# Top-32 attention joined to a capacity-dropping mixture of experts: the sign tile multiplied, the loop one unit deeper, reciprocals later, and three smaller edits

## The chip, the cores and the metric

The program runs on one core of a Trainium2 chip. The metric is the device time of one execution in microseconds. Five engines work side by side, each taking its own instructions in order: TensorE (PE, with its weight loads shown as PEld), VectorE (DVE), ScalarE (ACT), GpSimd (POOL) and SyncE (SP, which here only issues DMA). TensorE's results go to PSUM, of which this kernel uses all eight banks in the attention loop.

## The reference, cut to what matters

Attention keeps the 32 largest scores of every query row, and its result feeds a routed expert layer in which every one of eight experts serves at most 80 tokens.

```python
# q, k, v: (8 batches, 8 heads, 576 rows, 64), float32
scores = scale * np.matmul(q, k.transpose(0, 1, 3, 2))
kth = np.partition(scores, -32, axis=-1)[..., -32:-31]       # the 32nd largest of each row
scores = np.where(scores >= kth, scores, -1e9)
attn = np.exp(scores - max); attn /= attn.sum(-1) + 1e-9     # (cut: keepdims)
x = (attn @ v) as (4608 tokens, 512)                         # (cut: transpose, reshape)
# experts: w_gate (512, 8), w1 (8, 512, 1024), w2 (8, 1024, 512), capacity 80
expert = argmax(x @ w_gate); gate = softmax(x @ w_gate)[expert]
for e in range(8):
    tok = the 80 tokens of expert e with the largest gate
    out[tok] = gate[tok] * (relu(x[tok] @ w1[e]) @ w2[e])     # all other rows are zero
```

## The kernel before

The attention works through 32 pairs of heads (n). A pair has five blocks of query rows (t): four of 128 rows, each counted as two units (h = 0, 1, one for each head), and a last block of 64 rows in which both heads share the 128 partitions as one unit. That makes 9 units a pair and 288 units in all. Each unit is a tile of 128 rows by 576 scores, and `step(i)` issues one step of a software pipeline: work for unit i and for its neighbours, each at another stage.

For every unit VectorE must find the 32nd largest score of each row. It takes the 8 largest of six pieces of 96 scores (48 candidates), finds the 24th largest of these, removes from the row everything at or above it (tile y), takes the 8 largest of the rest, and picks the 32nd with the help of a count (cnt) that ScalarE makes.

```python
    def parts(self, i):                       # letter G of the step: six of these (a takes the end)
        for j in range(NG):
            nc.vector.max(out=cand[:, j, :], in_=s[:, j * S // NG : (j + 1) * S // NG])      # L208
            yield

    def search(self, i):                      # letters a b c d e y g h, one part at each yield
        ...
        for r in range(G0 // 8):              # 3 rounds: a, (b) c, (d) e
            nc.vector.max(out=dst, in_=cand)                                                 # L219
            if r == G0 // 8 - 1:              # after e: ScalarE's sign of (24th - s), summed into cnt
                sign = self.rows.tile([P, S], BF16, name="sign", tag="sign", bufs=1)
                nc.scalar.activation(sign, s, Act.Sign, bias=w9[:, 7:8], scale=-1.0, accum_out=cnt)   # L224
            yield
            if r < G0 // 8 - 1:
                nc.vector.match_replace(out=cand, in_to_replace=dst, in_values=cand, imm_value=LOW)   # L227
                yield
        y = self.rows.tile([P, S], F32, name="y", tag="y")
        nc.vector.scalar_tensor_tensor(out=y, in0=s, scalar=w9[:, 7:8], in1=s, op0=Alu.is_lt, op1=Alu.mult)  # L230
        yield                                 # y
        nc.vector.max(out=w9[:, 8:], in_=y)   # g                                             # L232
        yield
        nc.vector.scalar_tensor_tensor(out=pick, in0=past, scalar=cnt, in1=w9[:, 7:], ...)   # h, L235: the threshold
        yield

    def below(self, i):                       # letter m: GpSimd's mask
        nc.gpsimd.tensor_scalar(self.mask[i], self.s[i], self.thr[:, i : i + 1], None, op0=Alu.is_lt)   # L243
```

TensorE and ScalarE do the rest for each block. `front` makes the scores (TensorE into the tile sp, L196; ScalarE copies them to s, L201). `turn_w` turns s (L275) and adds the mask (L280) into the PSUM tiles ab and cc; ScalarE takes the exponential (L282, L284). `back` multiplies by v (L298) into a part of cc, with the row sums beside the products. `over` is VectorE's reciprocal of those sums (L310, the letter z), and `divide` ScalarE's scaling by it (L319). `turn` transposes the next pair's q and k. `norm`, once a pair, transposes the result (L173, L174), multiplies it by the gate weights (L336), and has VectorE add the logits (L345). The tile sp is a single buffer of four banks, and `front`, `turn` and two parts of `norm` all use it in turn.

```python
            back = dict(a=0, b=1, c=1, d=1, e=1, y=1, g=2, h=3, m=3)   # how many units behind each letter works
            for c in "GhmbGcGdGeGGgazy":                                 # VectorE's (and m: GpSimd's) order in a step
                ...
            if whole(i - 3):
                self.turn_w(*units[i - 3][:2])
            for u in drawn: self.divide(*u)                              # (cut)
            fronts = 0 <= i + 3 < NU and units[i + 3][2] != 1
            if not fronts and due: self.turn(due.pop()); busy = True     # (cut)
            for g in list(later): ...                                    # the parts of norm, in steps without front
            if fronts:
                self.front(*units[i + 3][:2])
            if whole(i - 4):
                self.back(*units[i - 4][:2]); drawn.append(...)
```

After the loop come the routing (`route`) and the experts. In the routing, TensorE runs 72 products of a zero tile with itself (L623) while VectorE finds each expert's 80th gate (L660, L662), then a few small products (L667, L676, L677), 48 weight loads with products for the list of chosen tokens (L692), and 36 more zero products. In the experts, `product` ends with one copy of the PSUM tile yp to SBUF, and `store` transposes that copy, scales it and writes the rows out:

```python
        def product(e):
            for d in range(HP):               # 4 column blocks of w2
                ... nc.tensor.matmul(ps[u : u + HF, d, :cap], ...)       # L766
            nc.scalar.copy(y_t[e], ps[:, :, :cap])                      # L769, 128 x 320
        def store(e):
            for d in range(HP):
                nc.tensor.transpose(ps[:cap, d * P : (d + 1) * P], yT[:, d, :], ident)   # L775
```

Of the kernel before, what the change touches and what calls it, by code (L numbers as in the profile page):

```python
# [9 lines left out]
F32 = mybir.dt.float32  # L10
BF16 = mybir.dt.bfloat16
# [15 lines left out]
def kernel(  # L27
# [11 lines left out]
    nc = tc.nc  # L39
# [18 lines left out]
    NG = 6  # L58
    G0 = 24
    TOP = 24  # L60
    WARM1, WARM2 = 72, 36
    UPP = 2 * NF + 1
    NU = NP * UPP

# [58 lines left out]
    class Attention:  # L123
# [62 lines left out]
        def front(self, n, t):  # L186

            qT, kT = self.turned[n]
            m = P if t < NF else TL
            i = n * UPP + 2 * t  # L190
            ps = self.four()
            for j in range(2):
                for h in range(2):
                    d = slice(D * h, D * h + D)
                    o = ps[:, 2 * h + j, :HS] if t < NF else ps[TL * h : TL * h + TL, j, :HS]
                    nc.tensor.matmul(o, lhsT=qT[d, t * P : t * P + m], rhs=kT[d, j * HS : (j + 1) * HS], start=True, stop=True)  # L196
            g = 2 if t < NF else 1
            s = self.rows.tile([P, 2 * S], F32, name="s", tag="s", bufs=2 if self.lean else 4)
            for h in range(g):
                self.s[i + h] = s[:, h * S : (h + 1) * S]  # L200
            nc.scalar.activation(s[:, : g * S].rearrange("p (j c) -> p j c", c=HS), ps[:, : 2 * g, :HS], Act.Copy, scale=TINY)  # L201
# [10 lines left out]
        def search(self, i):  # L212

            s, cand = self.s[i], self.top[i]
            top = self.top[i] = self.small.tile([P, G0 // 8 - 1, 8], F32, name="top", tag="top")
            w9 = self.small.tile([P, 16], F32, name="w9", tag="w9")
            for r in range(G0 // 8):
                dst = top[:, r, :] if r < G0 // 8 - 1 else w9[:, :8]
                nc.vector.max(out=dst, in_=cand)  # L219
                if r == G0 // 8 - 1:  # L220

                    sign = self.rows.tile([P, S], BF16, name="sign", tag="sign", bufs=1)
                    cnt = self.small.tile([P, 1], F32, name="cnt", tag="cnt")
                    nc.scalar.activation(sign, s, Act.Sign, bias=w9[:, 7:8], scale=-1.0, accum_out=cnt)  # L224
                yield
                if r < G0 // 8 - 1:
                    nc.vector.match_replace(out=cand, in_to_replace=dst, in_values=cand, imm_value=LOW)  # L227
                    yield
            y = self.rows.tile([P, S], F32, name="y", tag="y")
            nc.vector.scalar_tensor_tensor(out=y, in0=s, scalar=w9[:, 7:8], in1=s, op0=Alu.is_lt, op1=Alu.mult)  # L230
            yield
            nc.vector.max(out=w9[:, 8:], in_=y)  # L232
            yield
            pick = self.small.tile([P, TOP_K - G0 + 1], F32, name="pick", tag="pick")
            nc.vector.scalar_tensor_tensor(out=pick, in0=past, scalar=cnt, in1=w9[:, 7:], accum_out=self.thr[:, i : i + 1],  # L235
                                           op0=Alu.is_equal, op1=Alu.mult)
            yield

        def below(self, i):

            self.top.pop(i)
            self.mask[i] = self.rows.tile([P, S], BF16, name="mask", tag="mask", bufs=3)
            nc.gpsimd.tensor_scalar(self.mask[i], self.s[i], self.thr[:, i : i + 1], None, op0=Alu.is_lt)  # L243

        def search_all(self, i):

            s = self.s[i]
            top = self.top[i] = self.small.tile([P, TOP_K // 8, 8], F32, name="top", tag="top")
            scr = self.rows.tile([P, S], F32, name="y", tag="y")
            nc.vector.max(out=top[:, 0, :], in_=s)  # L250
            for r in range(1, TOP_K // 8):
                nc.vector.match_replace(out=scr, in_to_replace=top[:, r - 1, :], in_values=s if r == 1 else scr,
                                        imm_value=LOW)
                nc.vector.max(out=top[:, r, :], in_=scr)
            nc.vector.tensor_copy(self.thr[:, i : i + 1], top[:, TOP_K // 8 - 1, 7:8])
# [125 lines left out]
        def run(self, slow):  # L381

            units = []
            for n in range(NP):
                for t in range(NF):
                    units += [(n, t, 0), (n, t, 1)]
                units.append((n, NF, 2))
            first, second = {}, {}
            later = []
            due = []  # L390
            drawn = []
            ready = {}

            def whole(i):

                return 0 <= i < NU and units[i][2] > 0

            def step(i, last):
                if 0 <= i < NU:
                    n, t, h = units[i]  # L400
                    if t == 0 and h == 1 and 0 < n and n + 1 < NP:
                        self.load(n + 1, *divmod(n + 1, HP))
                    if t in (1, 3) and h == 0 and slow and n:
                        slow.pop(0)()
                    if t == 1 and h == 0 and n + 1 < NP:
                        due.append(n + 1)
                    first[i] = self.parts(i)

                back = dict(a=0, b=1, c=1, d=1, e=1, y=1, g=2, h=3, m=3)
                for c in "GhmbGcGdGeGGgazy":  # L410
                    if c == "G":
                        if 0 <= i < NU:
                            next(first[i])
                    elif c == "a":
                        if 0 <= i < NU:
                            next(first[i], None)
                            second[i] = self.search(i)
                            next(second[i])
                    elif c == "z":
                        for u in drawn:  # L420
                            self.over(*u)
                    elif c == "m":
                        if 0 <= i - back[c] < NU:
                            self.below(i - back[c])
                    elif i - back[c] in second:
                        next(second[i - back[c]])
                busy = False
                if whole(i - 3):
                    self.turn_w(*units[i - 3][:2])
                ends = []  # L430
                for u in drawn:
                    self.divide(*u)
                    if u[1] == NF:
                        ends.append(u[0])
                drawn.clear()
                fronts = 0 <= i + 3 < NU and units[i + 3][2] != 1
                if not fronts:
                    if due:
                        self.turn(due.pop())
                        busy = True  # L440
                for g in list(later):
                    if ready[g] and (fronts or busy) and not last:
                        continue
                    busy = busy or ready[g] == 1
                    ready[g] = next(g, None)
                    if ready[g] is None:
                        later.remove(g)
                for n in ends:
                    b, hp = divmod(n, HP)
                    later.append(self.norm(n, b, hp, b % 2, 2))  # L450
                    ready[later[-1]] = 0
                if fronts:
                    self.front(*units[i + 3][:2])
                if whole(i - 4):
                    self.back(*units[i - 4][:2])
                    drawn.append(units[i - 4][:2])

            with tc.manual_schedule():
                self.load(0, 0, 0)
                self.load(1, *divmod(1, HP))  # L460
                nc.sync.dma_start(wg, moe_w_gate.rearrange("(c p) e -> p c e", p=P))
                self.turn(0)
                i = -3
                while i < NU + 5 or later:
                    step(i, i > NU + 5)
                    i += 1
            assert not slow and not due

# [228 lines left out]
    def finish(wpool, full):  # L697
# [60 lines left out]
        def product(e):  # L758

            hT = h_t.pop(e)  # L760
            ps = ps_y.tile([P, HP, P], F32, name="yp", tag="y")
            for d in range(HP):
                for f in range(FK):
                    for u in range(0, P, HF):
                        o = d * P + u
                        nc.tensor.matmul(ps[u : u + HF, d, :cap], lhsT=w2_t[e][:, f, o : o + HF], rhs=hT[:, f, :],  # L766
                                         start=(f == 0), stop=(f == FK - 1))
            y_t[e] = fs.tile([P, HP, cap], F32, name="yT", tag="yT")
            nc.scalar.copy(y_t[e], ps[:, :, :cap])  # L769

        def store(e):
            ps = ps_x.tile([P, 512], F32, name="yx", tag="x")
# [103 lines left out]
```

## Time and profile before

| what | value | from |
|---|---|---|
| time | 1120.3 us, median of 3 (1116.78 to 1120.64) | the times |
| span of the profiled execution | 1118.8 us | page, first line |
| VectorE busy | 972.1 us, 87% | page, part 1 |
| TensorE busy | 926.0 us, 83% | page, part 1 |
| ScalarE busy | 714.0 us, 64% | page, part 1 |
| GpSimd busy | 515.7 us, 46% | page, part 1 |
| chain that ended last | DVE 47%, PE 28%, issue 11%, ACT 10% | page, part 4 |

How to read it: the busy shares are averages over the whole span. The slices of part 2 of the page split it in time: VectorE stands at 9 (90% or more) in 33 of the 35 slices that the attention loop fills (5 in the first, 8 in one other), and at 1 to 2 in the routing and the experts, where TensorE has the work. In the table of groups (part 5), a row names the source line, the engine and the operation, then the tiles written and read, their shapes, how often it ran, the busy time, the mean of one in ns, and the idle time of that engine just ahead of it with what ended it. An instruction's duration in the trace is longer than the time after which the next one of the same engine starts, since successive instructions overlap at their ends; the timeline shows both.

### The profile page before, as it was taken

How to read it: one execution, taken by the hardware profiler on the slowest of the kernel's cores; microseconds unless marked ns; L12 is line 12 of the kernel's file. 1: busy time of each engine (PE TensorE's matmuls, PEld its weight loads, DVE VectorE, ACT ScalarE, POOL GpSimd, SP SyncE). 2: the span in 40 equal slices, each digit the busy share in tenths (PEclk: the TensorE clock that was granted, in tenths of full speed). 3: DMA queues.
4: the chain of work that ended last, by engine and by line, in shares of the span. 5: the costliest groups of instructions: out<-in, count | busy, mean ns of one | idle time of the engine just before them, and what ended most of it. 6: DMA issues, size and time to landing. Idle time of an engine off the chain costs nothing.

```text
span 1118.8 us, 35976 instructions
## 1 busy us (share of the span) xinstructions
PE 926.0 (83%) x13353; PEld 755.2 (68%) x13353; DVE 972.1 (87%) x5213; ACT 714.0 (64%) x1534; POOL 515.7 (46%) x332
## 2 busy tenths in 40 slices
PE   6888888888788888888888888888788888768997
PEld 3666666666667666666667666676666666657896
DVE  5999999999999999999999999999899999962111
ACT  4777767777677777776676777777677767610110
POOL 2555554545545545554445554555455545511111
PEclk9999989999999989998899999999899989987999
DMA  4144443233322223233323311111111110042831
GB/s 102 43 118 111 119 119 82 81 82 81 82 53 65 68 70 82 75 80 81 81 81 82 82 44 34 43 33 35 34 44 44 44 45 12 13 162 68 330 131 28
DMA packets 167896, 85.79 MB, mean 77 GB/s; under 512 B 117792, under 2 KB 154656, under 8 KB 167712
## 3 DMA queue, kind: packets, MB, share of 16 engines
q1 hardware_dynamic: 166688, 80.78, 26.3%
q0 software_dynamic: 1024, 2.62, 0.8%
q8 instruction: 107, 1.75, 0.6%
q14 instruction: 77, 0.63, 0.2%
HBM read 63.19 MB, written 20.19 MB: 75 GB/s over the span
## 4 chain that ended last, share of the span: by engine, by line
DVE 47%; PE 28%; issue 11%; ACT 10%; POOL 2%; DMA 1%; SPq 0%; DVEq 0%; POOLq 0%; ACTq 0%
DVE cand L208 17%; DVE y L230 7%; PE cc L298 7%; DVE w L232 6%; DVE cand L227 6%; ACT s L201 5%; DVE top L219 4%; PE sp L173 3%; PE yp L766 3%; PE ab L275 3%; ACT wT L284 3%; DVE pick L235 2%; POOL mask L243 2%; DVE w L219 2%; PE sp L196 1%
## 5 line engine op out<-in xcount | busy, mean ns | idle before, releaser
L243 POOL TENSOR_SCALAR mask<-s,thr_all 128x576 bf16<-128x576 f32 x288 | 496.2, 1723 | 482.7 <-DVE cand L227 460.9
L208 DVE MAX8 cand<-s 128x8 f32<-128x96 f32 x1728 | 397.0, 243 | 9.0 <-ACT s L201 9.0
L224 ACT ACTIVATE sign<-s,w 128x576 bf16<-128x576 f32 x288 | 226.2, 785 | 119.0 <-DVE w L219 114.6
L298 PEld LDWEIGHTS cc<-vb,wT 128*64 128x64 f32 x5760 | 216.7, 148 | 36.8 <-ACT wT L284 19.9
L298 PE MATMUL cc<-vb,wT 128*64 128x65 f32 x5760 | 238.6, 235 | 2.6 <-ACT wT L284 1.2
L230 DVE SCALAR_TENSOR_TENSOR y<-s,w 128x576 f32<-128x576 f32 x288 | 229.1, 795 | 0.0
L232 DVE MAX8 w<-y 128x8 f32<-128x576 f32 x288 | 212.8, 739 | 0.0
L196 PE MATMUL sp<-kT,qT 64*128 64x288 f32 (+1 forms) x1280 | 204.4, 439 | 5.0 <-ACT kT L184 2.5
L275 PE MATMUL ab<-ident,s 128*128 128x128 f32 x1152 | 185.5, 291 | 1.2 <-ACT wT L284 1.2
L201 ACT ACTIVATE s<-sp 128x1152 f32<-128x1152 f32 (+1 forms) x160 | 166.8, 1042 | 16.6 <-PE sp L196 16.4
L275 PEld LDWEIGHTS ab<-ident,s 128*128 128x128 f32 x1152 | 134.9, 148 | 25.4 <-ACT wT L284 15.3
L284 ACT ACTIVATE wT<-ab 128x1024 f32<-128x1024 f32 (+1 forms) x160 | 150.6, 941 | 0.1
L280 PEld LDWEIGHTS <-mask 128*128 128x128 bf16 x1440 | 94.3, 99 | 73.6 <-POOL mask L243 71.5
L196 PEld LDWEIGHTS sp<-kT,qT 64*128 64x128 f32 (+1 forms) x1280 | 106.8, 181 | 43.6 <-ACT s L201 4.1
L282 ACT ACTIVATE wT<-cc 128x256 f32<-128x256 f32 (+1 forms) x160 | 58.8, 368 | 107.1 <-PE cc L280 107.1
L280 PE MATMUL cc<-minus,mask 128*128 128x128 bf16 x288 | 64.2, 223 | 62.0 <-POOL mask L243 62.0
L219 DVE MAX8 top<-cand 128x8 f32<-128x48 f32 x576 | 108.8, 189 | 0.1
L227 DVE MATCH_REPLACE8 cand<-top,cand 128x48 f32<-128x48 f32 x576 | 108.5, 188 | 0.0
L280 PE MATMUL ab<-minus,mask 128*128 128x128 bf16 x1152 | 102.8, 220 | 0.0
L319 ACT ACTIVATE xn<-cc,z_all 128x64 f32<-128x64 f32 (+1 forms) x320 | 82.9, 317 | 1.9 <-DVE z_all L310 1.8
L275 PE MATMUL cc<-ident,s 128*128 128x128 f32 x288 | 81.1, 282 | 0.0
L173 PE MATMUL sp<-ident,xn 128*128 128x128 f32 x128 | 26.7, 344 | 42.4 <-ACT s L201 42.4
(185 smaller groups left out, 842.7 us busy)
## 6 DMA issues: line engine op xcount, KB each, us to landing
w<-in_moe_w_dram SPq DMA_DIRECT2D x32, 512.0 KB, 4.0
w<-in_moe_w_dram SPq DMA_DIRECT2D x8, 2048.0 KB, 12.9
out_dram<-zero SPq DMA_DIRECT2D x9, 1024.0 KB, 5.6
qn<-in_q_dram SPq DMA_DIRECT2D x64, 128.0 KB, 3.7
kn<-in_k_dram SPq DMA_DIRECT2D x64, 128.0 KB, 3.0
vb<-in_v_dram SPq DMA_DIRECT2D x64, 128.0 KB, 2.8
xd<-xn SPq DMA_DIRECT2D x32, 256.0 KB, 2.3
qn<-in_q_dram SPq DMA_DIRECT2D x32, 32.0 KB, 3.4
```

The lines of the kernel that those rows point to most:

```text
L196: nc.tensor.matmul(o, lhsT=qT[d, t * P : t * P + m], rhs=kT[d, j * HS : (j + 1) * HS], start=True, stop=True)
L201: nc.scalar.activation(s[:, : g * S].rearrange("p (j c) -> p j c", c=HS), ps[:, : 2 * g, :HS], Act.Copy, scale=TINY)
L208: nc.vector.max(out=cand[:, j, :], in_=s[:, j * S // NG : (j + 1) * S // NG])
L219: nc.vector.max(out=dst, in_=cand)
L224: nc.scalar.activation(sign, s, Act.Sign, bias=w9[:, 7:8], scale=-1.0, accum_out=cnt)
L230: nc.vector.scalar_tensor_tensor(out=y, in0=s, scalar=w9[:, 7:8], in1=s, op0=Alu.is_lt, op1=Alu.mult)
L232: nc.vector.max(out=w9[:, 8:], in_=y)
L243: nc.gpsimd.tensor_scalar(self.mask[i], self.s[i], self.thr[:, i : i + 1], None, op0=Alu.is_lt)
L275: nc.tensor.matmul(dst[h][c], lhsT=sc[:, keys[c]], rhs=ident, start=c == 0 or (c == NF and h == 0), stop=False, is_transpose=True, skip_gr ...
L280: nc.tensor.matmul(dst[h][c], lhsT=mk[:, keys[c]], rhs=minus, start=False, stop=True, skip_group_check=True)
L284: nc.scalar.activation(wT[:, : g * NF, :], ab.rearrange("p h c r -> p (h c) r")[:, : g * NF, :], Act.Exp, scale=scale / TINY)
L298: nc.tensor.matmul(cc[r : r + TL, o], lhsT=wT[:, j * NF + c if c < NF else 2 * NF + j, r0 : r0 + TL], rhs=vb[:, c, h, :], start=(c == 0), ...
```

## The change

Six edits. First, y becomes the product of the scores and the sign tile that ScalarE makes anyway: where the score is below the 24th largest it is multiplied by 1, at the 24th by 0, and above by -1, so that none of the first 24 is among the next 8 largest. This makes VectorE's instruction one of two tensors, with no per-partition scalar, and makes it depend on ScalarE. Second, to leave time for that, the pipeline becomes one unit deeper: y works two units behind instead of one, and all that follows one further; scores are made four units ahead instead of three (s gets five buffers, sign two, y one). Third, the reciprocals (z) move behind y in VectorE's order, and on TensorE the scores and the product by v come ahead of `turn` and `norm`; loads are issued for two pairs ahead. Fourth, the last unit's mask is made by VectorE. Fifth, the first set of zero products is 100 instead of 72. Sixth, the copy of the expert's product is made in two halves, each as soon as its two column blocks are done.

```diff
-    WARM1, WARM2 = 72, 36
+    WARM1, WARM2 = 100, 36
...
-            s = self.rows.tile([P, 2 * S], F32, name="s", tag="s", bufs=2 if self.lean else 4)
+            s = self.rows.tile([P, 2 * S], F32, name="s", tag="s", bufs=2 if self.lean else 5)
...
-                    sign = self.rows.tile([P, S], BF16, name="sign", tag="sign", bufs=1)
+                    sign = self.rows.tile([P, S], BF16, name="sign", tag="sign")
...
-            y = self.rows.tile([P, S], F32, name="y", tag="y")
-            nc.vector.scalar_tensor_tensor(out=y, in0=s, scalar=w9[:, 7:8], in1=s, op0=Alu.is_lt, op1=Alu.mult)
+            y = self.rows.tile([P, S], F32, name="y", tag="y", bufs=1)
+            nc.vector.tensor_tensor(out=y, in0=s, in1=sign, op=Alu.mult)
...
-            nc.gpsimd.tensor_scalar(self.mask[i], self.s[i], self.thr[:, i : i + 1], None, op0=Alu.is_lt)
+            engine = nc.vector if i == NU - 1 else nc.gpsimd
+            engine.tensor_scalar(self.mask[i], self.s[i], self.thr[:, i : i + 1], None, op0=Alu.is_lt)
...
-                    if t == 0 and h == 1 and 0 < n and n + 1 < NP:
-                        self.load(n + 1, *divmod(n + 1, HP))
+                    if t == 2 and h == 1 and n + 2 < NP:
+                        self.load(n + 2, *divmod(n + 2, HP))
...
-                    if t == 1 and h == 0 and n + 1 < NP:
+                    if t == 0 and h == 0 and n + 1 < NP:
                         due.append(n + 1)
...
-                back = dict(a=0, b=1, c=1, d=1, e=1, y=1, g=2, h=3, m=3)
-                for c in "GhmbGcGdGeGGgazy":
+                back = dict(a=0, b=1, c=1, d=1, e=1, y=2, g=3, h=4, m=4)
+                for c in "GhmbGcGdGeGGgayz":
...
-                if whole(i - 3):
-                    self.turn_w(*units[i - 3][:2])
+                if whole(i - 4):
+                    self.turn_w(*units[i - 4][:2])
... (divide as before)
+                busy = 0 <= i + 4 < NU and units[i + 4][2] != 1
+                if busy:
+                    self.front(*units[i + 4][:2])
+                if whole(i - 5):
+                    self.back(*units[i - 5][:2])
+                    drawn.append(units[i - 5][:2])
+                if due and not busy:
+                    self.turn(due.pop())
+                    busy = True
                 for g in list(later):        # parts of norm
...
-                if fronts:
-                    self.front(*units[i + 3][:2])
-                if whole(i - 4):
-                    self.back(*units[i - 4][:2])
-                    drawn.append(units[i - 4][:2])
... (in product)
-            y_t[e] = fs.tile([P, HP, cap], F32, name="yT", tag="yT")
-            nc.scalar.copy(y_t[e], ps[:, :, :cap])
+                if d % 2:
+                    nc.scalar.copy(y_t[e][:, d - 1 : d + 1, :], ps[:, d - 1 : d + 1, :cap])
```

More of the change, by code (lines that the diff above doesn't have):

```diff
@@ L248, in search_all @@
             top = self.top[i] = self.small.tile([P, TOP_K // 8, 8], F32, name="top", tag="top")
-            scr = self.rows.tile([P, S], F32, name="y", tag="y")
+            scr = self.rows.tile([P, S], F32, name="y", tag="y", bufs=1)
             nc.vector.max(out=top[:, 0, :], in_=s)
@@ L426, in step @@
                         next(second[i - back[c]])
-                busy = False
-                if whole(i - 3):
-                    self.turn_w(*units[i - 3][:2])
-                ends = []
+                if whole(i - 4):
+                    self.turn_w(*units[i - 4][:2])
                 for u in drawn:
                     self.divide(*u)
-                    if u[1] == NF:
-                        ends.append(u[0])
+                ends = [n for n, t in drawn if t == NF]
                 drawn.clear()
[L436 to L440, printed above, removed]
+                busy = 0 <= i + 4 < NU and units[i + 4][2] != 1
[7 more added lines that the diff above has]
+                    busy = True
                 for g in list(later):
-                    if ready[g] and (fronts or busy) and not last:
+                    if ready[g] and busy and not last:
                         continue
@@ L462, in run @@
                 self.turn(0)
-                i = -3
-                while i < NU + 5 or later:
-                    step(i, i > NU + 5)
+                i = -4
+                while i < NU + 6 or later:
+                    step(i, i >= NU + 6)
                     i += 1
@@ L761, in product @@
             ps = ps_y.tile([P, HP, P], F32, name="yp", tag="y")
+            y_t[e] = fs.tile([P, HP, cap], F32, name="yT", tag="yT")
             for d in range(HP):
```

## The prediction

> **What bounds the kernel now.** I read the busy digits by slice first, then the windows of the middle, then VectorE's groups and waits, and the timeline last. The windows view gives, after each stretch and its length, the busy time of PE, PEld, DVE, ACT and POOL with the number of instructions, then the granted TensorE clock, the DMA share and GB/s:
>
> ```profile
> 300.00:500.00 200.00, 165.88 (x2259) 133.46 (x2259) 194.01 (x1058) 145.52 (x313) 103.39 (x60) 0.95 0.29 76
> 500.00:700.00 200.00, 167.31 (x2241) 134.23 (x2242) 192.16 (x1049) 142.68 (x308) 101.59 (x59) 0.93 0.27 69
> ```
>
> VectorE is busy 96 to 97% of the attention loop; TensorE (83%) and ScalarE (72%) follow. So the loop lasts as long as VectorE's instructions, plus the 3 to 4% in which it stands still. Both can be read. From the table of groups:
>
> ```profile
> L230 DVE SCALAR_TENSOR_TENSOR y<-s,w 128x576 f32<-128x576 f32 x288 | 229.1, 795 | 0.0
> L232 DVE MAX8 w<-y 128x8 f32<-128x576 f32 x288 | 212.8, 739 | 0.0
> ```
>
> From the waits (engine, line, what it waited for: us in total, times, longest):
>
> ```profile
> DVE z_all L310 <- PE cc L298: 33.2, 39, 5.1
> PE sp L173 <- ACT s L201: 50.2, 48, 1.4
> PE sp L336 <- ACT s L201: 42.7, 30, 1.4
> ```
>
> VectorE has one wait of weight, the reciprocal L310 for the product by v, L298. Two of the 39 lie after the loop (5.05 and 0.98 us by the timeline, at 984.5 and 985.7), so 33.2 - 6.0 = 27 us lie in it. The other two rows say why TensorE is late: parts of norm wait for the score tile's one buffer, until ScalarE has emptied it. The timeline shows such a wait turn into VectorE's (start, duration, then the instruction; in brackets the idle time before):
>
> ```profile
> 677.87 0.76 PE L336 MATMUL sp<-wg,xT 128*64 128x8 f32 x20 [1.43 <-ACT s L201]
> ...
> 678.47 1.36 PE L298 MATMUL cc<-vb,wT 128*64 128x65 f32 x40
> ...
> 679.95 0.17 DVE L310 RECIPROCAL z_all<-cc 128x2 f32<-128x2 f32 x1 [0.83 <-PE cc L298]
> 680.04 0.80 DVE L230 SCALAR_TENSOR_TENSOR y<-s,w 128x576 f32<-128x576 f32 x1
> 680.76 0.25 DVE L208 MAX8 cand<-s 128x8 f32<-128x96 f32 x1
> ```
>
> TensorE stood 1.43 us in L336, the product by v queued behind it, and 0.83 us of that reached VectorE. The last two lines show a second thing: y lasts 0.80 us, but the next instruction starts after 680.76 - 680.04 = 0.72 us. That start-to-start time counts, not the duration.
>
> [...]L682, 384 elements, lasts 558 ns[...], and L345, 40 elements, 190 ns[...]. [...] I expect nothing from sign being bf16. No run so far shows such a mixed pair. [...]the mask's 1723 ns should stay. [...]after 3.52 us of idle before L667 the clock granted from 1009.3 to 1018.5 is 0.50.
>
> **The change part by part.**
>
> *The sign product.* [...]start-to-start is what I need. Of L230 it is 0.72. L232, also over 576 elements and without a scalar operand, starts at 602.58 and is followed at 603.24: 0.66. L345, a tensor_tensor of 40 elements, starts at 975.61 and is followed at 975.72: 0.11[...]. I take 0.67: 288 x 0.05 = **14.4 us** less, all on the engine that bounds.
>
> *The order.* Two things help the wait of 27 us. The reciprocal comes after y, thus 0.67 us later, and on TensorE the product by v goes ahead of turn and norm, so that L336 and L173 can wait for ScalarE without holding it. With the deeper loop, the nine-step period spreads TensorE's work too: before, one step had the turned weights, the next pair's transposes and the product by v together; after, that step has only the last two. Not all goes: the granted clock averages 0.93 to 0.95, so about a tenth of the time is at half clock, and there TensorE falls behind by a microsecond or two (L298 x40 took 2.36 instead of 1.34 us at 610.77 in the chain). I leave 4 us of waits: **23 us** less.
>
> *The deeper loop.* Its start costs nothing that I can see, since the first scores are made in the same order. At the end, y of the last two units waits for a further step. Between the last 24th maximum and the next-to-last threshold, VectorE before runs one L232 and one L230 (0.66 + 0.72); after, two L232, two products and one more L235 (2 x 0.66 + 2 x 0.67 + 0.2 = 2.9). That threshold comes 1.5 us later, and what follows it is GpSimd's 1.72 us mask, the exponentials and the last block. The last mask on VectorE saves the second of two masks that GpSimd now runs back to back (978.65, 3.42 us for two), but the last block waits then for PSUM tile ab (at 982.05, 1.17 us on L284) anyhow. Net **1.5 us more**.
>
> *The zero products.* 72 last 8.92 us from 996.90, to 1005.82; L667 starts at 1009.34 when VectorE's L665 is done. At the mean of 124 ns, 28 more end at 1009.3: they fill the gap and hold up L667 by at most a few tenths. The gain is the clock: the 48 products L692 took 6.59 us, all at 0.50, and a full clock would nearly halve them. [...]I expect full clock for the small products (0.3 us) and about a third of L692 (1.2 us): **1.5 us** less.
>
> *The halves.* At the end TensorE waits twice for the whole copy: L775 has 0.58 us before it at 1105.44 and at 1111.23, behind a copy of 0.43 us. With halves the last copy is perhaps 0.3 us, and two of the four transposes run ahead of it. **0.5 us** less in all; the other experts' copies are hidden, as L775 comes a whole expert later.
>
> Loads two pairs ahead: one wait of 4.0 us for qn and little else is in the trace, so next to nothing.
>
> Sum: -14.4 - 23 + 1.5 - 1.5 - 0.5 = -38 us, from 1120.3 to **1082 us** (0.966).
>
> **The rivals.**
>
> *A new wait for ScalarE.* y now needs sign. For it: ScalarE waited for L219 before sign only 93 of 288 times, so in two thirds of the units it comes late to it. Against: sign is issued at the last 24th maximum (605.33 to 605.51; sign starts 605.61 and lasts 0.78, and 0.19 for its sum), while y of that unit comes at the end of the next step (the slots of y stand at 606.60 and 609.77), 4.2 us after that maximum. ScalarE would have to lag by about 3 us; it was at most one exponential pair and a score copy behind in the stretches that I read. Each 0.05 us of mean wait would cancel the gain of the product: then about 1096.
>
> *TensorE becomes the bound.* 167 of 200 us are 83%; over a loop 4% shorter it is 87%, with stretches at half clock. If the waits of 27 us only move elsewhere (to the masks' transposes, then to s), the product's 14 us remain: about 1105.
>
> *The product isn't shorter.* If tensor_tensor starts its successor after 0.72 like L230, the order alone gives 1096; were the mixed pair slower than that, by 0.1 us a unit, 29 us would be lost and 1110 would remain.
>
> *Nothing waits at all.* Then 4 us more are gained, and with L692 wholly at full clock 2 more: about 1076.
>
> **Range and chances.** The product is the surest part, 11 to 17 us. The waits give 15 to 27. The rest lies between -5 and +3. So 1071 to 1094 should hold it 8 times in 10. Faster by over 2% means under 1097.9; for that the order alone nearly suffices, and only a new wait of size undoes both: 0.93.
>
> **What the profile after would show.** L230 as TENSOR_TENSOR with[...] a start-to-start of 0.67; the row of L310 waiting for L298 down from 33 to 10 us or less, the end included; no row of L230 waiting for ACT L224 above 3 us; VectorE busy 98 to 99% in the middle windows; L243 still 1.72 us; TensorE's waits for ACT s L201 still there, but without effect; the gap before L667 under 1 us and L692 under 6 us; two rows of the copy to yT. Wrong would be a tensor_tensor of over 0.72 start to start, sign arriving late, or VectorE below 97%.

## The result, and the profile after

The changed kernel takes **1109.7 us** (median; 1108.5 to 1110.41) against 1120.3: a ratio of 0.991, 95% interval 0.989 to 0.993. It is faster, but by 11 us and not by 38, and outside the range of the prediction.

The windows of the kernel after, the two of the middle as in the prediction and then three stretches behind the loop: from the last unit's 24th maximum to the first product of the routing, the routing to the first turned rows, the experts to the end. Columns as before.

```profile
300.00:500.00 200.00, 171.67 (x2331) 133.91 (x2332) 199.93 (x1087) 147.42 (x320) 105.05 (x62) 0.97 0.28 72
500.00:700.00 200.00, 172.22 (x2317) 135.10 (x2317) 199.83 (x1080) 147.31 (x318) 104.96 (x61) 0.97 0.26 68
...
957.31:975.69 18.38, 11.34 (x176) 10.23 (x176) 8.29 (x35) 7.30 (x20) 6.11 (x12) 0.87 0.18 54
975.69:1005.91 30.22, 26.47 (x228) 22.29 (x229) 17.49 (x57) 0.00 (x0) 3.12 (x3) 0.75 0.35 130
1005.91:1108.49 102.58, 85.58 (x2115) 79.59 (x2113) 11.40 (x24) 11.66 (x32) 12.23 (x13) 0.97 0.42 148
```

The same three stretches of the kernel before:

```profile
976.72:991.83 15.11, 8.49 (x155) 7.45 (x156) 5.98 (x28) 6.35 (x18) 6.17 (x12) 0.89 0.22 71
991.83:1024.38 32.55, 25.28 (x201) 21.68 (x202) 17.57 (x57) 0.00 (x0) 3.13 (x3) 0.68 0.31 117
1024.38:1118.83 94.45, 83.43 (x2115) 78.56 (x2113) 11.40 (x24) 10.40 (x24) 12.27 (x13) 0.98 0.45 161
```

These windows cut the span where the parts begin, so their differences add up: loop 957.31 - 976.72 = -19.4 us, its end +3.3, the routing -2.3, the experts +8.1; together -10.3, the difference of the spans. Two things stand out. VectorE is busy in 199.9 of 200 us, so the standing still is gone, and yet the loop gained only 19.4 us. And the experts, in which nothing but a copy was changed, are 8 us longer.

The groups and the waits of the kernel after:

```profile
L230 DVE TENSOR_TENSOR y<-s,sign 128x576 f32<-128x576 f32 x288 | 218.5, 759 | 3.9 <-ACT sign L224 3.6
L232 DVE MAX8 w<-y 128x8 f32<-128x576 f32 x288 | 213.6, 742 | 0.0
```

```profile
DVE z_all L312 <- PE cc L300: 6.7, 3, 4.5
DVE y L230 <- ACT sign L224: 3.6, 3, 2.4
...
PE yp L765 <- ACT yT L768: 8.9, 8, 2.1
```

The product lasts 759 ns, where the old instruction lasted 795; the waits at the reciprocal (L312 here) are down from 33.2 to 6.7 us; sign comes late three times only. What takes the time back is in none of these rows. It is seen in the timeline, VectorE alone, of one unit:

```profile
501.08 0.74 DVE L232 MAX8 w<-y 128x8 f32<-128x576 f32 x1
501.74 0.19 DVE L219 MAX8 top<-cand 128x8 f32<-128x48 f32 x1
501.92 0.76 DVE L230 TENSOR_TENSOR y<-s,sign 128x576 f32<-128x576 f32 x1
```

The same place in a unit of the kernel before that has no reciprocal between:

```profile
602.58 0.73 DVE L232 MAX8 w<-y 128x8 f32<-128x576 f32 x1
603.24 0.18 DVE L219 MAX8 top<-cand 128x8 f32<-128x48 f32 x1
603.35 0.79 DVE L230 SCALAR_TENSOR_TENSOR y<-s,w 128x576 f32<-128x576 f32 x1
```

L219 lasts 0.18 to 0.19 us in both, but start to start it cost 0.11 before. Now y starts 0.18 behind it, and as the busy bar of L219 just fills that gap, no view of busy or idle time counts it. The median from L219 to y is 0.186 us, where it was 0.109 (over the 130 units in which no reciprocal came between). The view of the source line names the cause:

```profile
L230 DVE TENSOR_TENSOR y<-s,sign x288: 757/759/762, 19.9 to 960.1; 128x576 f32<-128x576 f32 x144
L230 DVEq EVENT_SEMAPHORE  x287: 21/21/21, 22.9 to 960.1; - x144
```

The second row is an instruction in VectorE's queue that is not in the program text: a wait of 21 ns, 287 times, once ahead of every y but the first. y now waits for two things, ScalarE's sign and VectorE's own L232, which must have finished reading the one buffer of y before it is written again. The trace tells which of the two waits the instruction is: in every unit it starts 38 or 39 ns after the end of L232, and in the median y starts 45 ns after its end, so it is the wait for L232. The theory that I tested: this second wait stands as an instruction of its own ahead of y and costs 0.077 us a unit, 22 us in all, and y's single buffer makes it. A second theory: in the experts the products of the second half wait for the copy of the first.

### The profile page after: what moved, and what is told of

It reads as the page before. It is cut to its first block, busy times and chain, and to the rows that moved or that the text cites. A ratio compares the mean times of both kernels' runs of the same rounds, so it can differ in the third digit from the quotient of the medians.

```text
span 1108.5 us, 36039 instructions
## 1 busy us (share of the span) xinstructions
PE 936.7 (85%) x13381; PEld 745.3 (67%) x13381; DVE 978.4 (88%) x5214; ACT 711.1 (64%) x1542; POOL 513.4 (46%) x331
## 4 chain that ended last, share of the span: by engine, by line
DVE 84%; PE 12%; ACT 2%; another core or an unknown queue 1%; issue 0%; DMA 0%; POOL 0%; SPq 0%; POOLq 0%; DVEq 0%; ACTq 0%
DVE cand L208 25%; DVE y L230 19%; DVE w L232 17%; DVE cand L227 9%; DVE top L219 6%; DVE pick L235 3%; PE yp L765 3%; DVE w L219 3%; PE warm L621 2%; DVE z_all L312 1%; PE sp L196 1%; PE cc L300 1%; PE acc L690 0%; PE ab L277 0%
## 5 line engine op out<-in xcount | busy, mean ns | idle before, releaser
L245 POOL TENSOR_SCALAR mask<-s,thr_all 128x576 bf16<-128x576 f32 x287 | 494.0, 1721 | 465.8 <-DVE cand L227 455.9
L208 DVE MAX8 cand<-s 128x8 f32<-128x96 f32 x1728 | 399.2, 245 | 9.4 <-ACT s L201 9.4
L300 PEld LDWEIGHTS cc<-vb,wT 128*64 128x64 f32 x5760 | 213.5, 146 | 65.6 <-ACT wT L286 41.1
L300 PE MATMUL cc<-vb,wT 128*64 128x65 f32 x5760 | 236.0, 233 | 2.8 <-ACT wT L286 2.8
L196 PE MATMUL sp<-kT,qT 64*128 64x288 f32 (+1 forms) x1280 | 211.2, 451 | 14.7 <-ACT part L344 6.1
L230 DVE TENSOR_TENSOR y<-s,sign 128x576 f32<-128x576 f32 x288 | 218.5, 759 | 3.9 <-ACT sign L224 3.6
L232 DVE MAX8 w<-y 128x8 f32<-128x576 f32 x288 | 213.6, 742 | 0.0
L277 PE MATMUL ab<-ident,s 128*128 128x128 f32 x1152 | 176.9, 282 | 1.8 <-ACT wT L286 1.7
L196 PEld LDWEIGHTS sp<-kT,qT 64*128 64x128 f32 (+1 forms) x1280 | 109.0, 184 | 54.9 <-ACT part L344 8.0
L277 PEld LDWEIGHTS ab<-ident,s 128*128 128x128 f32 x1152 | 128.5, 142 | 25.3 <-ACT wT L286 15.9
L219 DVE MAX8 top<-cand 128x8 f32<-128x48 f32 x576 | 110.4, 192 | 0.1
L282 PE MATMUL ab<-minus,mask 128*128 128x128 bf16 x1152 | 110.1, 220 | 0.0
L235 DVE SCALAR_TENSOR_TENSOR pick<-past,cnt,w 128x9 f32<-128x9 f32 x288 | 60.8, 211 | 0.0
```

The lines of the kernel that those rows point to most:

```text
L230: nc.vector.tensor_tensor(out=y, in0=s, in1=sign, op=Alu.mult)
L245: engine.tensor_scalar(self.mask[i], self.s[i], self.thr[:, i : i + 1], None, op0=Alu.is_lt)
L277: nc.tensor.matmul(dst[h][c], lhsT=sc[:, keys[c]], rhs=ident, start=c == 0 or (c == NF and h == 0), stop=False, is_transpose=True, skip_gr ...
L282: nc.tensor.matmul(dst[h][c], lhsT=mk[:, keys[c]], rhs=minus, start=False, stop=True, skip_group_check=True)
L300: nc.tensor.matmul(cc[r : r + TL, o], lhsT=wT[:, j * NF + c if c < NF else 2 * NF + j, r0 : r0 + TL], rhs=vb[:, c, h, :], start=(c == 0), ...
```

## The experiments

Each kernel is named by what differs from the kernel after, unless said otherwise; all were timed in three rounds beside the kernel before. That kernel took 1121.0 us beside the first set (`y_two_bufs`, `stt_one_buf`, `whole_copy`, `y2_whole`), 1117.8 beside the second (`y2_late_halves`, `y2_whole_stt`, `y2_norm_first`, `y2_z_first`) and 1118.5 beside the rest, so a difference of under 3 us between kernels of different sets says little.

**Two buffers for y.** The reciprocals are kept for 8 pairs instead of 32 to make room; the step in the experts that looks at the smallest of all reciprocals (`judge`) then leaves out those of the first 24 pairs.

```diff
-            y = self.rows.tile([P, S], F32, name="y", tag="y", bufs=1)
+            y = self.rows.tile([P, S], F32, name="y", tag="y")
```

> The changed kernel with two buffers for y instead of one (to make room, the reciprocals are kept for 8 pairs instead of 32). Theory 'one buffer': y must wait until L232 has finished reading the y before it, which costs 0.077 us in every unit (from L219's start to y's 0.186 instead of 0.109 us); then that start-to-start falls back to 0.11, a step without reciprocal from 3.215 to 3.14 us, and the time falls by 20 to 22 us to about 1089. Rival 'sign': it is the wait for another engine's sign that costs it; then the start-to-start stays at 0.18 and the time at 1109.

1082.8 us, 26.9 less than the change as it came (ratio to before 0.966, 0.964 to 0.969). The timeline of one unit:

```profile
503.26 0.75 DVE L232 MAX8 w<-y 128x8 f32<-128x576 f32 x1
503.92 0.20 DVE L219 MAX8 top<-cand 128x8 f32<-128x48 f32 x1
504.02 0.75 DVE L230 TENSOR_TENSOR y<-s,sign 128x576 f32<-128x576 f32 x1
```

L219 to y is 0.10 again, though y still waits for sign: the rival falls. The gain was larger than expected because y itself also costs less with two buffers, 0.657 us start to start instead of 0.676. Together 0.096 x 288 = 27.6 us, which is also the difference of the two profiled spans (1108.5 - 1080.9). The single buffer lengthens the old instruction in the same way (next experiment), so this part does not come from the second wait; why it does so no run tells.

**The old instruction with one buffer.** y by compare and multiply with the per-partition scalar, in the new order: it has the wait for L232 but none for sign.

```diff
-            nc.vector.tensor_tensor(out=y, in0=s, in1=sign, op=Alu.mult)
+            nc.vector.scalar_tensor_tensor(out=y, in0=s, scalar=w9[:, 7:8], in1=s, op0=Alu.is_lt, op1=Alu.mult)
```

> The changed kernel with y made by the old instruction (the compare and multiply of s by itself, with a per-partition scalar), y still in one buffer, the copy still in halves. It waits for VectorE's own L232 alone and no more for the sign. Theory 'the reader must finish': from L219's start to y's 0.15 to 0.19 us as with the product, a step 0.04 us longer than in the changed kernel, 1121 us. Rival 'two waits on one instruction' (the product has one for sign and one for y's reader, and the second is handled as an instruction of its own): 0.11 us, a step 0.036 us shorter, about 1099.

1104.7 us, between the two. The median from L219 to y decides: it is 0.118 us.

```profile
503.61 0.75 DVE L232 MAX8 w<-y 128x8 f32<-128x576 f32 x1
504.27 0.20 DVE L219 MAX8 top<-cand 128x8 f32<-128x48 f32 x1
504.39 0.82 DVE L230 SCALAR_TENSOR_TENSOR y<-s,w 128x576 f32<-128x576 f32 x1
```

y starts 504.39 - 504.36 = 0.03 us after L232 ends; in the kernel after it was 501.92 - 501.82 = 0.10. The one wait for L232, riding on y, costs 0.009 us (0.118 instead of 0.109), and the view of this line has no EVENT_SEMAPHORE. So "the reader must finish" is too simple: what costs is that beside the wait for sign this wait becomes an instruction of its own, which adds 0.07. The single buffer is not free here either, as y itself takes 0.735 us start to start, against 0.717 and 0.718 in the two kernels that have it in two buffers (`before` and `y2_whole_stt`), whatever the number of reciprocals kept: together 0.027 us a unit, 7.8 us in all, which puts the time above the 1099 us of the rival. No run has the product in one buffer without the wait for sign; that it takes two waits to make the extra instruction is inferred from where it appears and where it does not.

**One maximum between L232 and y.** The copy whole (see below), y in one buffer, and VectorE's order changed.

```diff
-                for c in "GhmbGcGdGeGGgayz":
+                for c in "GhmbGcGdGeGgGyaz":
```

> The changed kernel with the copy whole, y in one buffer, and VectorE's order in a step changed so that one 96-element maximum stands between L232 and y, and the first 24-maximum round behind y. Theory 'the second wait is exposed': y's own wait for L232 is handled as an instruction of its own, and what it costs depends on how long before y the reader L232 ends; with 0.16 us more between them, some 0.03 us of the 0.077 remain, and the time is 14 us under the whole copy's 1105.2, about 1091. Rival 'a second wait costs 0.077 wherever it stands': 1105.

1089.8 us, 15.4 less than the same kernel with the order as it came (`whole_copy`), 13.7 of it in the loop by the two profiles, and without a byte of memory. The wait is still there:

```profile
500.66 0.74 DVE L232 MAX8 w<-y 128x8 f32<-128x576 f32 x1
501.32 0.24 DVE L208 MAX8 cand<-s 128x8 f32<-128x96 f32 x1
501.50 0.76 DVE L230 TENSOR_TENSOR y<-s,sign 128x576 f32<-128x576 f32 x1
```

y starts 0.84 us after the start of L232, as in the kernel after. But the time is used: L208 would hold y back to 0.66 + 0.16 = 0.82 anyway, so 0.026 us are exposed instead of 0.077. In both kernels y starts 0.104 us after the end of its reader in the median: the cost is a distance from the reader, and what lies in it is free.

**The copy whole.**

```diff
-                if d % 2:
-                    nc.scalar.copy(y_t[e][:, d - 1 : d + 1, :], ps[:, d - 1 : d + 1, :cap])
+            nc.scalar.copy(y_t[e], ps[:, :, :cap])      # after the loop over d
```

> The changed kernel with the copy of the expert's product in one piece again. Theory 'interleaved halves': the products of the second half wait for the copy of the first, as they write the tile that it reads, and that makes the experts 8 us longer; then TensorE's wait on L765 for the copy goes and the time falls by 8 to 9 us to about 1101. Rival: the experts are longer through instruction or weight transfers that fall otherwise; then the time stays within 2 us of 1109.7.

1105.2 us, 4.5 less, half of what was expected. TensorE's wait for the copy is gone, which in the kernel after looks like this:

```profile
1028.10 2.44 PE L765 MATMUL yp<-hT,w 128*64 128x80 f32 x64
...
1032.15 0.29 ACT L768 COPY yT<-yp 128x160 f32<-128x160 f32 x1 [4.13 <-remote]
...
1032.49 2.44 PE L765 MATMUL yp<-hT,w 128*64 128x80 f32 x64 [1.96 <-ACT yT L768]
```

The 64 products of two column blocks, then nothing until ScalarE has copied them, then the other 64. The products of the second half write other columns of yp than the copy reads, but the program has them wait for it. Here the copy comes 1.6 us late besides, for a reason that the profile doesn't name; in the last products the gap is 0.61 us, and eight of those make 4.9 us. The experts fall from 102.6 to 97.4 us, not to 94.5; nor do they in any kernel below.

**Both.**

> Both: two buffers for y, and the copy in one piece. If the two costs are apart from each other (one in the loop, one after it) their gains add: about 1080. If the faster loop lets TensorE's waits come back at the reciprocal (rival 'TensorE close behind'), the sum is short by 5 to 15 us: 1085 to 1095, with waits of L312 for L300 above 10 us.

1076.8 us (0.961, 0.958 to 0.963): 6.0 less than with two buffers alone. The two costs add, and no wait of TensorE's comes back (L312 for L300: 4.9 us, all after the loop). The next ones are compared with this one, except `before_order`.

**Halves, both after the products.**

```diff
+            for d in range(0, HP, 2):                   # after the loop over d
+                nc.scalar.copy(y_t[e][:, d : d + 2, :], ps[:, d : d + 2, :cap])
```

> The changed kernel with two buffers for y, and the expert's copy still in two halves, but both issued after all four column blocks, so that no product waits for a copy. Theory 'interleaved halves': it was the second half's products behind the first copy that cost 5 to 6 us; then the experts are no longer than with the whole copy (96.9 us from the first turned rows to the end) and shorter by 0.5 us, as two of the four transposes run ahead of the second copy: about 1076.3. Rival: two copies instead of one cost it by themselves; then about 1082.

1076.1 us; the experts take 96.5 us, against 96.9 with the one copy of `y2_whole`. So two copies cost nothing by themselves; it is their place between the products. TensorE's wait at the end falls from 0.58 to 0.45 us, too little to be seen in the time.

**What the product is worth.** Two buffers, the copy whole, y by the old instruction.

> Two buffers for y, the copy whole, and y made by the old instruction with the per-partition scalar. It tells what the product by the sign is worth where it has no second wait: from L219 to the instruction after y it takes 0.109 + 0.717 us instead of 0.109 + 0.657, 288 times, 17 us: about 1094. If TensorE or ScalarE stood close behind VectorE, less: 1080 to 1088.

1090.3 us: 13.5 more than `y2_whole`, 13.7 more than `y2_z_first`, which was timed beside it. That is the product's gain where it has no second wait. Start to start y takes 0.718 us here and 0.657 as a product, 17.6 us over 288 units, of which the three waits for sign at the start (3.6 us) take back about a fifth. The prediction had put the gain at 14.4, with a smaller step (0.05) and no wait: that the two agree is in part luck.

**Which part of the order.** Three kernels, of which the last is the kernel before with TensorE's order alone.

```diff
+                # y2_norm_first: front(i + 4) and back(i - 5) moved behind turn and norm
-                for c in "GhmbGcGdGeGGgayz":
+                for c in "GhmbGcGdGeGGgazy":           # y2_z_first
+                # before_order: kernel before, front(i + 3) and back(i - 4) moved ahead of turn and norm
```

> Two buffers for y, the copy whole, and on TensorE turn and norm again ahead of the scores and the product by v, the reciprocals still behind y. If it was TensorE's order that took away the 27 us of waits at the reciprocal, most of them return (15 us or more, 1092 or more). If the deeper loop and the late reciprocal do it alone, within 3 us of 1076.8.

> Two buffers for y, the copy whole, and the reciprocals again ahead of y, TensorE's order as changed. If the late reciprocal is what took the waits away, 0.66 us come back at each of the 30 or so late products by v: up to 20 us. If TensorE's order does it, within 2 us of 1076.8.

> The kernel before with one thing changed: on TensorE the scores and the product by v come ahead of turn and norm, at the old depth and with everything else as it was. If TensorE's order alone removes the waits at the reciprocal, the 27 us of the loop go: about 1093 to 1097. If the deeper loop is needed for it (the step that has the turned weights, the transposes and the product by v together), half or less goes: 1105 or more.

The first took 1097.2 us, 20 more; the second 1076.6, the same; the third 1116.8, no gain that can be told (ratio to before 0.999, 0.997 to 1.0005). So the late reciprocal does nothing beside the other two, and neither TensorE's order nor the deeper loop removes the waits by itself. Added up as far as its start-to-start exceeds the median, the reciprocal's delay in the loop is 31.0 us before, 26.9 with the order alone, 15.4 with the depth and norm first, and none with both. Why not, the waits say. With norm first, in the deeper loop:

```profile
PE sp L173 <- ACT s L201: 86.2, 61, 1.6
...
DVE z_all L312 <- PE cc L300: 21.1, 22, 4.4
```

With the new order at the old depth:

```profile
DVE z_all L310 <- PE cc L298: 28.6, 28, 5.0
...
PE sp L196 <- ACT kT L184: 40.6, 32, 1.3
```

In the first, norm's transposes stand ahead of the product by v and wait for the one score tile. In the second they no longer do (their weight loads wait 7.4 us for s in all, 68.7 before), but once in every pair the next scores come right behind turn, wait 1.3 us for ScalarE's copy of the turned keys, and the product by v stands behind them. In the deeper loop the turned weights stand between turn and the next scores, and no product by v stands behind those scores: L196 waits for kT twice instead of 32 times.

**The small edits.**

```diff
-    WARM1, WARM2 = 100, 36
+    WARM1, WARM2 = 72, 36                              # y2_warm72
-            engine = nc.vector if i == NU - 1 else nc.gpsimd
+            engine = nc.gpsimd                          # y2_mask_pool
```

> Two buffers for y, the copy whole, and 72 zero products instead of 100. If the 28 gave the routing its 2.3 us (32.55 us before, 30.23 with 100, from the first product of the routing to the first turned rows), they come back: about 1079. The experts, 2 to 3 us longer than in the kernel before though nothing of them differs, tell whether the number of instructions ahead of them matters: if so they fall back to 94.5.

> Two buffers for y, the copy whole, and the last mask on GpSimd again. If the last block waits for PSUM tile ab in any case, the end of the loop stays as it is, 1076.8 within 1 us; if the mask on VectorE was what kept the deeper loop's end short, 1 to 2 us more.

With 72 zero products the routing is 2.7 us longer, as expected, but the experts are 1.7 us shorter, and the time is 1076.6: the 28 products gain nothing that the time shows. The other profiles agree that the experts go with the number of zero products: where no copy is in their way they take 94.5, 95.1 and 95.2 us behind 72 of them (`before`, `before_order`, `y2_warm72`) and 95.8 to 97.4 behind 100 (eight kernels). Why, no view tells. The last mask on GpSimd gave 1075.3, so the one on VectorE gains nothing either.

## Why the prediction was wrong, point by point

- **The sign product, -14.4 us: the step that failed.** Its own start-to-start was right (0.67 foretold, an estimate beside the 0.66 measured on L232; 0.676 measured in the kernel after), and with two buffers the product was worth 13.5. But the change list had y in one buffer, and I gave that no cost. From L219 to the end of y a unit took 0.109 + 0.717 us before and 0.186 + 0.676 after: 0.036 x 288 = 10.4 us more instead of 14.4 less. That is 25 of the 28 us by which I missed. The other misses nearly cancel, which is luck: +8.6 in the experts, +3.6 of waits for sign and +1.8 at the end of the loop against -10.4 at the reciprocal and -0.8 in the routing.
- **The halves, -0.5 us: wrong in sign.** I read the copies as hidden and did not ask what the products would wait for. Placed between the products they cost 4.5 to 6.0 us. With the copies out of the way the experts are still 1.3 to 3.0 us longer than the 94.5 of before wherever 100 zero products run ahead of them, and within 0.7 with 72 (95.1 where they were not changed at all, 95.2 in `y2_warm72`). So I had counted the gain of the 28 products in the routing and not this loss behind it; its cause stays open.
- **The waits at the reciprocal, -23 us: right in kind, too small, one reason wrong.** All of the loop's went. By difference they were worth -19.4 - 10.4 - 3.6 = -33 us, the last number being the three waits for sign, and 31 added up start to start; both lie outside the 15 to 27 that I gave. The view of waits, from which I took 27, counts only what lies beyond the end of the instruction before. And I had named the late reciprocal first, which does nothing beside the other two. It is the order on TensorE and the depth, and both are needed.
- **The end of the loop, +1.5: it was +3.3,** and 1.9 to 4.3 over all the deeper kernels, less where the granted clock was higher (17.0 us at 0.94 with both corrections, against 18.4 at 0.87). **The zero products, -1.5:** -2.3 in the routing, so foretold in kind, but not visible in the time of the whole. L692 took 4.74 us at a granted clock of 0.73, against 6.59 at 0.50; that about a third of it would come at full clock was my estimate, shown by no trace of the kernel before. **GpSimd's mask** stayed, at 1.72 us.
- **The rivals.** ScalarE's sign was late three times at the start, 3.6 us in all. TensorE stood at 86% busy in the middle, and at 88% with two buffers, and did not become the bound. The rival that came true was not on my list: a wait of VectorE for itself. The list has the measured time, 1110 us, under "the product isn't shorter", but only by luck: the product was shorter, and a pair slower by 0.1 us than the 0.72 named there would have given 1096 + 29 = 1125.
- **The sign that misled.** I had written that VectorE at 98 to 99% would show the change at work. It was at 100%, with a tenth of a microsecond lost in every unit, because durations overlap and hide such gaps; with two buffers for y it is at 100% too, and 27 us faster.

## What to carry to other kernels

When a change reduces a buffer from two to one on the engine that bounds, count the waits of the instruction that writes it: here the single buffer cost 0.03 us each time with one wait and 0.10 with two, 27 us in all; a second buffer gave all of it back, an instruction moved in between about half. Read start-to-start times in the timeline and the queue's own rows, not the busy share, where an engine seems full. And split an eviction only behind the last product that writes the tile: here a copy between two halves of the products made them wait, 0.61 us in the last ones.

## What I had not expected of the hardware

The second wait of one instruction. From L219 to y it is 0.109 us without the wait for L232 (`before`) and 0.118 with it alone (`stt_one_buf`). With the wait for sign beside it, it is 0.186 us (`after`), and a wait of 21 ns stands as an instruction of its own. The product of an fp32 and a bf16 tile of 576 elements lasts 759 ns with y in one buffer and 730 with two (`y_two_bufs`). The mask that takes GpSimd 1721 ns took VectorE 520 ns in the kernel after.
